# Loading the last w4 row of each partition by thirteen small transfers on ten or eight partitions each

## The chip, the cores and the metric

The kernel runs on one core of one Trainium2 chip. The metric is the device time of one execution in microseconds; for the kernel before, it was 1304.69 us, the median of three runs that lay between 1304.60 and 1304.81 us. A separate profiled execution gives the trace that is read below; its own time is in the table.

A core has engines that run side by side: TensorE (PE, matrix products), VectorE (DVE), ScalarE (ACT), GpSimd (POOL) and SyncE (SP, which here only issues transfers). Transfers between the large memory (HBM) and the on-chip memory (SBUF, 128 partitions) are carried by 16 DMA engines. Engines wait for each other, and for transfers, on semaphores; a transfer raises its semaphore by 16 when all of it has landed.

## The reference

One decoding step for four sequences, in float32. `x` is 4 x 512. It is normalised to `xn`, and the output is `x + A(xn) + B(xn)`:

```
xn  = layernorm(x)
q   = xn @ wq               -> 4 batches, 32 heads, 128 each
p   = softmax(q . k_cache * 128**-0.5)     k_cache: 4 x 32 x 4096 x 128
A   = (p @ v_cache) @ wo                   v_cache the same size, wo: 4096 x 512
B   = xn + gelu(LN(xn) @ w3) @ w4          w3: 512 x 1792, w4: 1792 x 512
```

(The reference's mixer with w1 and w2 shifts the sequence by one or two places; a sequence of length one is shifted out, so its term is zero and the kernel doesn't load those weights.) Nearly all of the bytes are the two caches: 256 MiB each. Every byte of them is read once.

## The kernel before, in words

**Tiling.** The caches are cut into 32 groups of four heads (`NG = 32`). A group is 8 MiB: each of the 128 partitions holds one contiguous row of 64 KB. SBUF has three such slots. `S1` and `S0` take K groups by turns, `S2` takes V groups. VectorE multiplies K by the query and sums (lines 343 to 347), ScalarE takes exponentials (line 245), TensorE multiplies the weights with V (line 201, recorded as line 108, the helper that issues every matrix product).

**The transfers.** SyncE issues all large loads, in one written order, on one DMA queue (lines 127 to 157). In the loop it waits until a slot is free and issues the next 8 MiB load into it. Each slot's wait ends while earlier loads are still under way, so loads queue up behind each other. After the loop it issues, in this order:

- line 146, w3 (3584 KB), and line 148, the rows 0 to 3 of w4 (1024 KB);
- lines 150 and 152, the last V group in two parts (3072 and 5120 KB), each after a wait for its part of the slot;
- line 153, the rows 4 to 13 of w4 (2560 KB);
- after one more wait (line 154, the K slot `S0` has been read), lines 155 to 157: wo in six pieces. wo has 32 rows of 2 KB in each partition, and the pieces hold 14, 8, 5, 3, 1 and 1 of them (`PIECES`, line 73).

**w4's layout.** w4 is 1792 x 512, so each partition holds 14 rows of 512 numbers, one behind the other in HBM: 28 KB for each partition, 2 KB for each row (`NF = 14`, line 147). Row 13 is the last row that this text speaks of.

**What waits for them.** TensorE, after the last group's products (block `pe_rest`, line 213), waits until both w4 loads have landed (line 215, 32 on semaphore `s_w4`), multiplies the gelu values with w4 (14 products, 28 records of the trace, lines 217 to 219), then forms the transposed attention output X (line 221), and then takes wo piece by piece: line 373 waits for piece n's own semaphore, and lines 374 to 382 multiply it. The first 27 rows of wo go through the accumulator `y`, rows 27 to 31 straight into `total`. When the last piece is through, VectorE and ScalarE copy `total` out (lines 391 and 393), and SyncE and ScalarE write the two halves of the result to HBM (line 396).

**x.** The input x (4 rows of 2 KB) is loaded at the start by ScalarE's own DMA queue, into four partitions (line 226). It is the only load of the kernel that goes to fewer than 128 partitions; the two result transfers read four partitions each.

Of the kernel before, what the change touches and what calls it, by code (L numbers as in the profile page):

```python
# [13 lines left out]
P = 128  # L14
# [6 lines left out]
def decode_block(ctx: ExitStack, tc: tile.TileContext, x, k, v, wq, wo, w3, w4, out):  # L21
# [5 lines left out]
    NF = F // P  # L27
# [39 lines left out]
    def sem(name):  # L67
        return tc.alloc_semaphore(name)

    def take(e, s, n=1):  # L70
        e.wait_ge(s, n).then_inc(s, -n)  # L71
# [2 lines left out]
    CUT = 27  # L74
    SUM = 30
    GF = 12
    s_x, s_v, s_q, s_w3, s_w4 = (sem(n) for n in ("sx", "sv", "sq", "sw3", "sw4"))
    s_k = [sem(f"sk{n}") for n in range(2)]
    s_wo = s_k + [s_x] + [sem(f"swo{n}") for n in range(3)]
# [16 lines left out]
    w4_sb = S1[:, NC * F:w34].rearrange("p (m n) -> p m n", m=NF)  # L96
# [10 lines left out]
    def mm(e, o, l, r, start, stop):  # L107
        return e.matmul(o, l, r, start=start, stop=stop)  # L108

    nc.vector.addr_align(128, offset=4, max_nops=0)  # L110
    with tc.tile_critical(no_gpsimd_drain=True), nc.Block(no_gpsimd_drain=True) as block:

        @block.sync
        def _(e):
            def src(flat, g):
                return flat[g] if isinstance(g, int) else flat[bass.ds(g, 1)].rearrange("g p r -> (g p) r")

            def load_k(g, n):
                e.dma_start(KS[n][:, :], src(kf, g)).then_inc(s_k[n], 16)

            def load_v(g):
                take(e, v_free)
                e.dma_start(S2[:, :], src(vf, g)).then_inc(s_v, 16)

            FIRST, REST = slice(0, GF * 4 * DH), slice(GF * 4 * DH, ROW)
            wq_r = wq.rearrange("(p c) n -> p (c n)", p=P)
            e.dma_start(S2[:, FIRST], wq_r[:, FIRST]).then_inc(s_v, 16)
            e.dma_start(S2[:, REST], wq_r[:, REST]).then_inc(s_q, 16)
            for half, s in ((slice(0, ROW // 2), s_k[0]), (slice(ROW // 2, ROW), s_kh)):
                e.dma_start(S1[:, half], kf[0][:, half]).then_inc(s, 16)  # L130
            e.wait_ge(d_T, 1)
            load_k(1, 1)
            with nc.Fori(0, NG, 2, engines=[ET.SP]) as g:
                load_v(g)
                take(e, k_free)
                e.br_lt(g, NG - 2, on_true="sp_more", on_false="sp_next")
                with nc.body("sp_more", valid_engines=[ET.SP]):
                    after = nc.s_assert_within(g + 2, None, NG - 2,
                                               skip_runtime_bounds_check_because="the last turn skips this block")
                    load_k(after, 0)  # L140
                    load_v(after - 1)
                    take(e, k_free)
                    load_k(after + 1, 1)
                    nc.br("sp_next", engines=[ET.SP])
                nc.switch_bb("sp_next")
            e.dma_start(w3_sb, w3.rearrange("(p c) f -> p c f", p=P)).then_inc(s_w3, 16)
            w4_r = w4.rearrange("(p m) n -> p m n", p=P)
            e.dma_start(w4_sb[:, 0:4, :], w4_r[:, 0:4, :]).then_inc(s_w4, 16)
            e.wait_ge(v_half, NG)
            e.dma_start(S2[:, FIRST], vf[NG - 1][:, FIRST]).then_inc(s_v, 16)  # L150
            take(e, v_free)
            e.dma_start(S2[:, REST], vf[NG - 1][:, REST]).then_inc(s_q, 16)
            e.dma_start(w4_sb[:, 4:NF, :], w4_r[:, 4:NF, :]).then_inc(s_w4, 16)
            take(e, k_free)
            wo_r = wo.rearrange("(p c) n -> p c n", p=P)
            for n, (c0, c1) in enumerate(PIECES):
                e.dma_start(wo_sb[:, c0:c1, :], wo_r[:, c0:c1, :]).then_inc(s_wo[n], 16)  # L157
# [20 lines left out]
        @block.tensor  # L178
        def _(e):
            pe = [ET.PE]  # L180
            zero = e.zero_reg
            e.br_lt(zero, 0, on_true="pe_near", on_false="pe_far")
            with nc.body("pe_near", valid_engines=pe):
                with nc.Fori(0, NG + 1, 1, engines=pe) as g:
                    e.br_lt(g, NG, on_true="pe_turn", on_false="pe_mlp")
                    with nc.body("pe_mlp", valid_engines=pe):
                        e.wait_ge(s_w3, 16)
                        for c in range(NC):
                            for t in range(4):
                                i = mm(e, pb[32 * t:32 * t + 32, :FT], x1T[:, c, :], w3_sb[:, c, t * FT:(t + 1) * FT],  # L190
                                       c == 0, c == NC - 1)
                        i.then_inc(p_a, 1)
                        nc.br("pe_turn", engines=pe)
                    nc.switch_bb("pe_turn")
                    take(e, s_v, 16)
                    take(e, a_p)
                    for n in range(G4):
                        if n == GF:
                            take(e, v_rest)
                        t = n % 4  # L200
                        i = mm(e, pv[32 * t:32 * t + 32, :], pw[:, n, :], V[:, n // 4, t], n < 4, n >= G4 - 4)
                        if n == GF - 1:
                            i.then_inc(v_half, 1)
                    i.then_inc(p_a, 1)
                    mm(e, oz[:, HG:2 * HG], ones[:, :], rs[:, :], True, True).then_inc(v_free, 1)
                    take(e, a_p)
                    for m in range(4):
                        i = mm(e, oz[:, 0:HG], os[:, m, :], sel[:, HG * m:HG * m + HG], m == 0, m == 3)
                    i.then_inc(p_a, 1)
                e.br_lt(zero, 0, on_true="pe_far", on_false="pe_rest")  # L210
            with nc.body("pe_far", valid_engines=pe):
                e.br_lt(zero, 0, on_true="pe_rest", on_false="pe_near")
            nc.switch_bb("pe_rest")
            mm(e, total[:, 0:P], ident[:, :], base[:, :], True, False)
            e.wait_ge(s_w4, 32)
            take(e, d_p)
            for m in range(NF):
                t = m % 4
                mm(e, y[32 * t:32 * t + 32, :], gT[:, 32 * m:32 * m + 32], w4_sb[:, m, :], m < 4, False)
            take(e, d_p)  # L220
            mm(e, pb[:, 0:P], perm[:, :], Xt[:, :], True, True).then_inc(p_d, 1)
# [148 lines left out]
    with tc.tile_critical(no_gpsimd_drain=True):  # L370
        e = nc.tensor
# [57 lines left out]
```

## Time and profile before

| | |
|---|---|
| median of three runs | 1304.69 us (1304.60 to 1304.81) |
| the profiled execution's own time | 1304.76 us |
| its span, first to last instruction | 1302.8 us |
| busy: VectorE / TensorE / ScalarE | 1167.5 / 371.5 / 107.5 us |
| moved by DMA | 561.05 MB, 431 GB/s over the span |
| share of the 16 DMA engines' time that SyncE's queue (q1) filled | 99.6% |
| mean granted TensorE clock | 0.625 of full speed |

The profiled execution took 1.96 us more than its span: what lies before the first and after the last instruction. The sums of the prediction are made against the profiled execution, which lies 0.07 us above the median.

Read the profile in this way. The page shows the span in forty slices, with the busy share of each engine and of the sixteen DMA engines together. A view of DMA by stretch counts the packets that begin in a stretch; one packet is one contiguous row moved for one partition, or the four bytes by which a DMA engine reports on the semaphore that its share of a transfer has landed. The chain of waits goes back from the last instruction to what released each step. The timeline lists instructions in order, with the idle time before them and what ended it.

### The profile page before, as it was taken

The numbers are of one execution on the slowest core, as the hardware profiler recorded it, in microseconds if no ns is written. First come the engines' busy times: TensorE is split into PE (matmuls) and PEld (weight loads), VectorE is DVE, ScalarE is ACT, GpSimd is POOL, SyncE is SP. The second block draws the span as 40 slices with busy tenths as digits, with TensorE's granted clock in tenths as the row PEclk, the third lists the DMA queues.
The fourth block names the chain that finished last, engine by engine and source line by source line (L and its number), as shares of the span: only waits on it lengthen the run. The fifth ranks groups of instructions, "written<-read, shape, count | busy, mean of one in ns | idle before, by whom it ended". The sixth has DMA issues, their size and how long they took to land. (4 is left out here: it accounts for less than half of the span.)

```text
span 1302.8 us, 7122 instructions
## 1 busy us (share of the span) xinstructions
PE 371.5 (29%) x2608; PEld 131.0 (10%) x2608; DVE 1167.5 (90%) x337; ACT 107.5 (8%) x330; POOL 2.5 (0%) x10
## 2 busy tenths in 40 slices
PE   3032123333113333212333212333311333321356
PEld 1010001111001111001111000111100111100112
DVE  4999999999999999999999999999999999999970
ACT  1000000000000000000000000000000000000010
POOL 0000000000000000000000000000000000000000
PEclk9565566666566666556666556666656666656678
DMA  9999999999999999999999999999999999999998
GB/s 402 436 449 421 449 421 449 421 439 429 425 445 421 449 421 449 421 449 421 449 421 445 425 437 431 425 445 421 449 421 449 421 449 421 447 423 445 425 430 344
DMA packets 11115, 561.05 MB, mean 431 GB/s; under 512 B 1244, under 2 KB 1252, under 8 KB 1640
## 3 DMA queue, kind: packets, MB, share of 16 engines
q1 hardware_dynamic: 11096, 561.00, 99.6%
q8 instruction: 2, 0.03, 0.0%
q14 instruction: 1, 0.01, 0.0%
q10 hardware_dynamic: 16, 0.01, 0.0%
HBM read 561.00 MB, written 0.01 MB: 431 GB/s over the span
## 5 line engine op out<-in xcount | busy, mean ns | idle before, releaser
L108 PE MATMUL ps<-slot,pw 128*32 128x512 f32 x2112 | 310.8, 753 | 905.5 <-PEq L71 905.5
L347 DVE TENSOR_REDUCE sc<-slot 128x128 f32<-128x16384 f32 x32 | 551.0, 17220 | 4.2
L343 DVE TENSOR_TENSOR slot<-slot,qb 128x8192 f32<-128x8192 f32 x32 | 278.1, 8692 | 60.8 <-DVEq L71 60.1
L345 DVE TENSOR_TENSOR slot<-slot,qb 128x8192 f32<-128x8192 f32 x32 | 277.9, 8684 | 1.1 <-DVEq L71 1.1
L108 PEld LDWEIGHTS ps<-slot,pw 128*32 128x32 f32 x2112 | 84.5, 134 | 1105.3 <-issue 1105.3
L233 ACT COPY os<-ps 128x512 f32<-128x512 f32 x33 | 19.3, 585 | 898.1 <-ACTq L71 898.1
L245 ACT ACTIVATE pw<-sc,st 32x128 f32<-32x128 f32 x128 | 67.4, 527 | 211.6 <-ACTq L71 210.4
L108 PE MATMUL ps<-sel,os 128*128 128x4 f32 x264 | 33.9, 252 | 18.6 <-PEq L71 18.6
L108 PEld LDWEIGHTS ps<-sel,os 128*128 128x128 f32 x264 | 31.9, 191 | 20.5 <-issue 20.5
L245 ACT ACTIVATION_READ_ACCUMULATOR pw<-sc,st 32x1 f32 x128 | 23.5, 184 | 0.0
L364 DVE RECIPROCAL rec<-OS 128x128 f32<-128x128 f32 x1 | 1.0, 952 | 15.5 <-DVEq L71 15.5
L349 DVE TENSOR_REDUCE st<-sc 128x1 f32<-128x128 f32 x32 | 9.2, 286 | 4.7
L108 PE MATMUL ps<-rs,ones 128*128 128x4 f32 x66 | 12.7, 263 | 0.0
L108 PEld LDWEIGHTS ps<-rs,ones 128*128 128x128 f32 x66 | 9.8, 188 | 27.7 <-issue 27.7
L337 DVE COPY qx<-Q 128x128 f32 x32 | 7.3, 227 | 5.0 <-issue 4.7
L391 DVE COPY res<-ps 64x128 f32<-64x128 f32 x1 | 0.3, 283 | 12.7 <-PE ps L108 12.7
L340 DVE STREAM_TRANSPOSE qb<-qx 128x128 f32<-128x128 f32 x32 | 10.0, 312 | 1.1
L108 PE MATMUL ps<-slot,X 128*4 128x512 f32 (+1 forms) x94 | 9.0, 457 | 3.9 <-DMA slot<-in_A_wo_dram 3.9
L253 ACT COPY OS<-ps 128x8 f32 x32 | 5.3, 165 | 43.8 <-ACTq L71 43.8
L351 DVE STREAM_TRANSPOSE mt<-mx 128x32 f32<-128x32 f32 x32 | 6.8, 211 | 1.1
L352 DVE TENSOR_REDUCE st<-mt 128x1 f32<-128x32 f32 x32 | 5.9, 186 | 1.1
L350 DVE COPY mx<-st 128x32 f32<-128x32 f32 x32 | 5.8, 181 | 1.1
(57 smaller groups left out, 39.3 us busy)
## 6 DMA issues: line engine op xcount, KB each, us to landing
slot<-in_A_k_cache_dram SPq DMA_DIRECT2D x2, 4096.0 KB, 36.0
slot<-in_A_wq_dram SPq DMA_DIRECT2D x1, 5120.0 KB, 22.4
slot<-in_A_v_cache_dram SPq DMA_DIRECT2D x1, 5120.0 KB, 20.5
slot<-in_B_w_dram SPq DMA_DIRECT2D x1, 3584.0 KB
slot<-in_A_wo_dram SPq DMA_DIRECT2D x1, 3584.0 KB, 29.4
slot<-in_A_wq_dram SPq DMA_DIRECT2D x1, 3072.0 KB, 10.7
slot<-in_A_v_cache_dram SPq DMA_DIRECT2D x1, 3072.0 KB, 13.1
slot<-in_B_w_dram SPq DMA_DIRECT2D x1, 2560.0 KB, 26.3
```

The costliest lines, as they stand in the source:

```text
L108: return e.matmul(o, l, r, start=start, stop=stop)
L233: return e.copy(os[:, :, :], pv[:, :].rearrange("p (m d) -> p m d", m=4)).then_inc(a_p, 1)
L245: i = e.activation(o, sc[r, :].rearrange("p (a w t) -> p a t w", w=4, t=4), AF.Exp, bias=st[r, 1:2], scale=1.0, accum_out=rs[r, h:h + 1])
L337: own(e.tensor_copy(qx[:, :].rearrange("p (h r) -> p h r", h=4), Q[:, bass.ds(g + n, 1), :].rearrange("p o h -> p (o h)").unsqueeze(2) .to ...
L340: own(e.transpose(qb[:, :], qx[:, :]))
L343: mark(e.tensor_tensor(out=K[:, :C // 2, :], in0=K[:, :C // 2, :], in1=qw, op=ALU.mult))
L345: own(e.tensor_tensor(out=K[:, C // 2:, :], in0=K[:, C // 2:, :], in1=qw, op=ALU.mult))
L347: mark(e.reduce_sum(sc[:, :], K, axis=AX.X))
L349: own(e.reduce_max(st[:, 0:1], sc[:, :], axis=AX.X))
L350: own(e.tensor_copy(mx[:, :], st[:, 0:1].to_broadcast([P, 32])))
L351: own(e.transpose(mt[:, :], mx[:, :]))
L352: e.tensor_reduce(st[:, 1:2], mt[:, :], axis=AX.X, op=ALU.max, negate=True).then_inc(d_a, 1)
```

## The change

The load of w4's rows 4 to 13 is cut in two. Rows 4 to 12 (18 KB for each partition) are loaded by one transfer as before. Row 13 (2 KB for each partition) is loaded by thirteen transfers behind it: twelve that each take ten partitions which lie twelve apart (partitions r, r + 12, ..., r + 108 for r = 0 to 11) and one that takes the partitions 120 to 127. All are issued by SyncE on the same queue and raise the same semaphore. TensorE waits for 32 + 16 x 13 = 240 on it instead of 32. Nothing else differs: the bytes, their places in SBUF and the arithmetic are the same.

```
+    LAST = (*(slice(r, 120, 12) for r in range(12)), slice(120, P))
...
-            e.dma_start(w4_sb[:, 4:NF, :], w4_r[:, 4:NF, :]).then_inc(s_w4, 16)
+            e.dma_start(w4_sb[:, 4:NF - 1, :], w4_r[:, 4:NF - 1, :]).then_inc(s_w4, 16)
+            for rows in LAST:
+                e.dma_start(w4_sb[rows, NF - 1, :], w4_r[rows, NF - 1, :]).then_inc(s_w4, 16)
...
-            e.wait_ge(s_w4, 32)
+            e.wait_ge(s_w4, 32 + 16 * len(LAST))
```

## The prediction, made before the change was run

> **What bounds the kernel now.** I read the page first, for the shares of the span:
>
> ```profile
> span 1302.8 us, 7122 instructions
> PE 371.5 (29%) x2608; PEld 131.0 (10%) x2608; DVE 1167.5 (90%) x337; ACT 107.5 (8%) x330; POOL 2.5 (0%) x10
> ...
> DMA  9999999999999999999999999999999999999998
> ...
> q1 hardware_dynamic: 11096, 561.00, 99.6%
> ```
>
> The DMA engines are full from one end to the other; VectorE, the busiest compute engine, has 10% to spare. So the time is that of the bytes on sixteen DMA engines, and a change counts if it changes the moment at which the last of them is done. The chain of waits, from 1259 us on, says the same of the end:
>
> ```profile
> 1259.43 36.57 DMA slot<-in_A_wo_dram
> ...
> 1296.04 1.88 PE ps L108 x10
> ...
> 1297.96 1.69 PE ps L108 x48
> ...
> 1299.67 0.28 DVE res L391
> ```
>
> TensorE takes wo as it lands, and 0.5 us after the last product the result goes out. The timeline shows where TensorE stands idle for a piece of wo:
>
> ```profile
> 1288.08 3.61 PE L108 MATMUL ps<-slot,X 128*4 128x512 f32 x28 [1.42 <-DMA slot<-in_A_wo_dram]
> ...
> 1296.04 0.12 PEld L108 LDWEIGHTS ps<-slot,X 128*4 128x4 f32 x8 [2.11 <-DMA slot<-in_A_wo_dram]
> ...
> 1297.96 0.55 PEld L108 LDWEIGHTS ps<-slot,X 128*4 128x4 f32 x24 [0.96 <-DMA slot<-in_A_wo_dram]
> ...
> 1299.20 0.12 PEld L108 LDWEIGHTS ps<-slot,X 128*4 128x4 f32 x8 [0.26 <-DMA slot<-in_A_wo_dram]
> ```
>
> It waits for every piece, for the last one until 1299.20. A shift of all landings therefore passes to the end in full, later without limit, earlier up to about 1.4 us (at 1288.08 TensorE had been idle that long; beyond it X itself would be late).
>
> A load has landed when the slowest of its sixteen shares has. I looked at the last stretch with 2 KB packets, first by DMA share, then by packets (from 1297.87 to 1298.72 us):
>
> ```profile
> 1297.30:1297.87 0.57, 0.57 (x2) 0.00 (x0) 0.00 (x0) 0.00 (x0) 0.00 (x0) 1.00 0.35 126
> 1297.87:1298.72 0.85, 0.82 (x29) 0.66 (x32) 0.00 (x0) 0.59 (x1) 0.00 (x0) 1.00 0.06 24
> ```
>
> ```profile
> DMA packets 12, 0.02 MB, mean 24 GB/s; under 512 B 2, under 2 KB 2, under 8 KB 12
> ...
> q1 hardware_dynamic: 12, 0.02, 6.3%
> ```
>
> A share of 0.06 of sixteen engines is one engine. For the last 0.85 us of the weights **one DMA engine works alone**, on ten 2 KB rows and two landing reports; the other fifteen are done by 1297.87. Why it is late stands at the start. The packets that begin from 1.94 to 2.75 us, then those in five stretches of 0.01 us (from 3.42, 4.83, 5.74, 6.65 and 7.57 us):
>
> ```profile
> q1 hardware_dynamic: 15, 0.37, 164.0%
> q8 instruction: 1, 0.02, 9.8%
> q14 instruction: 1, 0.01, 5.0%
> ```
>
> ```profile
> q1 hardware_dynamic: 1, 0.02, 886.2%
> ...
> q1 hardware_dynamic: 1, 0.02, 570.0%
> ...
> q1 hardware_dynamic: 1, 0.02, 570.0%
> ...
> q1 hardware_dynamic: 1, 0.02, 575.0%
> ...
> q1 hardware_dynamic: 1, 0.02, 570.0%
> ```
>
> Fifteen engines begin their first row of wq; the sixteenth moves instructions and begins its first row only at 3.42 us (this packet takes 886% of 16 x 0.01 us = 1.42 us, the next ones 0.91 us). Since the queue never runs dry, it keeps that delay for 1295 us. That it is the same engine at both ends is inferred, not shown.
>
> **The change part by part.**
>
> *Bytes per DMA engine.* Each of the sixteen had 8 rows of 20 KB of this load and now has 8 of 18 KB: 16 KB less. The rate, while V and w4 are loaded (1253.2 to 1274 us), is
>
> ```profile
> DMA packets 321, 8.95 MB, mean 430 GB/s; under 512 B 33, under 2 KB 33, under 8 KB 33
> ```
>
> 430 / 16 = 26.9 GB/s for an engine, so 16,384 B less is **-0.61 us on all sixteen**.
>
> *Who gets the 128 short rows.* The one load to few partitions that the trace shows is that of x (5.4 to 7.6 us):
>
> ```profile
> DMA packets 54, 1.14 MB, mean 518 GB/s; under 512 B 4, under 2 KB 4, under 8 KB 8
> ...
> q10 hardware_dynamic: 8, 0.01, 1.1%
> ```
>
> Four rows, four landing reports: four engines with one row each, not sixteen. By this nearest row I take ten engines with one row each for a load of ten partitions, eight for the last. On which engines a load begins, the trace doesn't show: I take the same first ten each time, so that eight engines get 13 rows, two get 12, and **six get none**. (The other bound, rows spread evenly, is a rival below.)
>
> *Price of a short row.* The lone engine gives it: 6.3% of 16 x 0.85 us is 0.857 us for ten rows with their reports, 0.086 us each. Lower bound, bytes alone at 26.9 GB/s: 0.076. Upper bound, the x rows: 1.1% of 16 x 2.2 us is 0.39 us for four, 0.097. So eight engines get 13 x 0.086 - 0.61 = +0.51 us (0.38 to 0.65), two get 12 x 0.086 - 0.61 = +0.42 (0.30 to 0.55), six get -0.61.
>
> *The end.* It turns on whether the late engine is one of the six. The four engines with an x row aren't it: an x packet pushes the next row of its engine back by 0.09 us, and the late engine's rows begin 0.91, 0.91 and 0.92 us apart all through the stretch with the x packets. If loads to few partitions begin on the same engine, the four are among the ten, and of the twelve engines left six are relieved, four get +0.51 and two +0.42. Six relieved is the largest of the three groups, and my forecast: the late engine is done 0.61 us sooner; the others, at least 0.85 us ahead of it, are then late by at most 0.51 - 0.85 = -0.34 against the old end. The end moves by -0.34 if the next-latest is one of the eight, up to -0.61 if all late ones are relieved. I take **-0.40**, nearer to the first, since ten of sixteen are loaded.
>
> *Issue.* SyncE issues thirteen more transfers between line 153 and the wait of line 154, with wo's six behind them:
>
> ```profile
> 1253.24 0.43 SPq L153 DMA_DIRECT2D slot<-in_B_w_dram  x1
> 1258.58 2.70 SPq L157 DMA_DIRECT2D slot<-in_A_wo_dram  x6
> 1299.98 0.35 SPq L396 DMA_DIRECT2D out_dram<-res  x1
> ```
>
> ```profile
> L226 ACTq DMA_DIRECT2D slot<-in_A_x_dram x1: 563/563/563, 1.6 to 1.6; - x1
> ```
>
> A transfer of four partitions costs 0.35 us on SyncE's queue and 0.56 us on ScalarE's; with the 0.04 us between issues, thirteen cost 5.1 to 7.8 us, and wo is issued from 1258.8 to 1261.5 us on instead of 1258.58. What hides it is the load of w4 ahead of wo, issued at 1253.24 and landed 26.3 us later, at 1279.5:
>
> ```profile
> DMA to landing us min/median/max: 26.3/26.3/26.3
> ...
> 1282.61 3.63 PE L108 MATMUL ps<-slot 128*32 128x512 f32 x28
> ```
>
> The engines reach wo some 18 us after its issue, so nothing of 0.2 to 2.9 us is seen; without that cover it would be paid in full. Nothing else is queued on SyncE until the result goes out at 1299.98. ScalarE's and GpSimd's queues aren't passed.
>
> *TensorE's wait on w4.* It now needs all fourteen loads. They land 1279.5 + 0.51 = 1280.0 us, 1280.2 at the upper bound; TensorE starts on w4 at 1282.61, after other work. Cost nothing with 2.4 us of cover; without it, X and wo's products behind it would be late.
>
> *Sum.* 1304.76 (the profiled execution) - 0.40 = 1304.36; the median stands 0.07 lower, so **1304.3 us**.
>
> **The rivals.**
>
> *The late engine is one of the ten* (0.40). Then it gets +0.42 or +0.51 and nothing covers it: 1304.7 + 0.5 = 1305.2 us (0.30 to 0.65, so 1305.0 to 1305.3). For it: ten of sixteen get more. Against it: only the x argument, which takes four of the ten away.
>
> *A load of ten rows uses one or two engines* (0.06), and this makes it slower. Sixty rows on each of two engines are 60 x 0.080 (bytes and a little) = 4.8 us, with the last load's row +0.09, less 0.61: +4.3; those engines are 0.85 to 1.4 us ahead of the late one, so about +3.0, 1307.7 us. On one engine, 120 rows: 9.6 + 0.7 for reports and the last row - 0.61 - 1.1 = +8.6, 1313.3 us. It decides from some 30 rows on one engine. For it: the trace shows four rows on four engines, never ten on ten. Against it: that same row.
>
> *The short rows spread evenly* (0.05): 8 x 0.086 - 0.61 = +0.08 on all sixteen, 1304.8 us: the change does nothing.
>
> *Each short load costs a pause of its own* (0.02). The result's 4 KB take at most 1302.8 - 1299.98 = 2.8 us from issue to the end; thirteen in a row would be +36 us, 1341 us. Against it: the wo pieces of 256 KB. From 1297.96 to 1299.20 two of them land: 1.24 us for 524,288 B, which at 430 GB/s are 1.22 us. Back-to-back loads leave no pause. [...]
>
> **How the numbers follow.** Forecast 0.47, then 0.40, 0.06, 0.05, 0.02. A difference under 0.2% (2.6 us) can't be told from none here; forecast, late-engine rival and even spread are all inside, 0.92, and the other two are slower, 0.08. For a gain over 2.6 us no engine has the room, as bytes are unchanged: 0.01, taken from the middle. The forecast's own range: 1304.1 (-0.61) to 1304.6 (0.65 - 0.85 = -0.20, with a margin). The range given reaches over the first rival too, and up to one more fetch of instructions on the late engine, since SyncE's program grows: 16 KB, +0.61: 1305.3 + 0.6 = 1305.9. Low: 1304.1 less the 0.1 by which runs differ. So 1303.9 to 1306.0.
>
> **What would show each step.** In the trace after: 2 KB packets and landing reports begin only at w4's end, 128 more of the one and 128 of the other, if ten rows go on ten engines; far fewer reports if on one or two. At the end, the stretch in which one engine works alone shrinks from 0.85 us to 0.5 or less if it was relieved, and grows to 1.2 or more if not. SyncE issues thirteen loads of about 0.4 us each, and wo begins at 1259 to 1261.5. TensorE starts on w4 within 0.1 us of 1282.6; an idle stretch there, ended by w4, makes the cover wrong. Wrong altogether I am if the time leaves 1303.9 to 1306.0: then either the rows lie on few engines, or short loads cost more than their bytes.

## The result, and the profile after

The changed kernel takes **1306.79 us** (median of 22 runs, 1305.55 to 1307.37) beside 1304.77 us before (22 runs, 1304.42 to 1305.10): the ratio is **1.0013, 95% interval 1.0007 to 1.0019**, so it is slower by some 0.1 to 0.2%. I had forecast 1304.3 us and a range up to 1306.0. The runs don't lie around one value: 9 of the 22 are at 1305.6 to 1306.0 us, 13 at 1306.7 to 1307.4. The profiled execution, 1305.73 us with a span of 1303.9 us, is of the lower group, 0.97 us above the profiled execution of before.

The page of the changed kernel:

```profile
span 1303.9 us, 7135 instructions
...
DMA packets 11372, 561.06 MB, mean 430 GB/s; under 512 B 1372, under 2 KB 1380, under 8 KB 1896
...
q1 hardware_dynamic: 11352, 561.00, 99.6%
```

There are 128 more packets under 512 B than before (1372 to 1244) and 256 more under 8 KB: 128 short rows with 128 landing reports, one engine for each row, as forecast. The queue is as full as before, for the same bytes and a longer time.

SyncE's issues in the timeline, and the thirteen and the six by line:

```profile
1253.64 0.43 SPq L154 DMA_DIRECT2D slot<-in_B_w_dram  x1
1254.12 9.72 SPq L156 DMA_DIRECT2D slot<-in_B_w_dram  x13
1263.96 10.97 SPq L160 DMA_DIRECT2D slot<-in_A_wo_dram  x6
```

```profile
L156 SPq DMA_DIRECT2D slot<-in_B_w_dram x13: 469/708/927, 1254.1 to 1263.4; - x13
```

```profile
L160 SPq DMA_DIRECT2D slot<-in_A_wo_dram x6: 353/432/4770, 1264.0 to 1270.2; - x6
```

An issue took 0.71 us, not the 0.35 to 0.56 that I had taken from the rows of before. One issue of wo stood for 4.77 us, and what is left of the 10.97 us says that another stood for some 4.3. The wo issues ended at 1274.9 instead of 1261.3. The engines reach wo's first row at 1277, so this is still hidden: even the last issue is 2 us ahead of that, where it was 16 us before.

What is not hidden shows in six microseconds, from 1277 to 1283, in which the short rows and the first rows of wo run. Before, and then after:

```profile
DMA packets 109, 2.58 MB, mean 429 GB/s; under 512 B 16, under 2 KB 16, under 8 KB 16
```

```profile
DMA packets 328, 2.12 MB, mean 354 GB/s; under 512 B 139, under 2 KB 139, under 8 KB 262
...
q1 hardware_dynamic: 328, 2.12, 106.2%
```

The DMA engines are busy all the time (106%, since packets count where they begin) and move 0.45 MB less. At 430 GB/s that is **1.05 us of all sixteen engines**, and the profiled executions differ by 0.97 us. In the middle of it, from 1277.40 to 1278.22 us, nothing begins but short rows and reports:

```profile
DMA packets 126, 0.13 MB, mean 155 GB/s; under 512 B 64, under 2 KB 64, under 8 KB 126
...
q1 hardware_dynamic: 126, 0.13, 68.5%
```

68.5% of 16 x 0.82 us is 8.99 us for 62 rows with their reports: **0.145 us for a row**, not 0.086. The long rows are slow as well. Three views of 0.01 us of the changed kernel (from 1276.82, 1277.31 and 1277.39 us), then one of 0.02 us of the kernel before (from 1279.02 us):

```profile
q1 hardware_dynamic: 1, 0.00, 52.5%
...
q1 hardware_dynamic: 3, 0.02, 674.4%
...
q1 hardware_dynamic: 1, 0.03, 1093.1%
...
q1 hardware_dynamic: 2, 0.03, 337.8%
```

The first short row of all takes 0.084 us (52.5% of 0.16), about the price that I had forecast. An 18 KB row of w4 with two reports takes 1.08 us, where 18,432 B at 26.9 GB/s are an estimated 0.69. A 28 KB row of wo takes 1.75 us; before, such a row and a report together took 1.08. The engine of this 28 KB row has no short rows: no engine can have had twelve of them, some 1.0 us at 0.084 us each, behind it 0.57 us after the first began. So the short rows also slow engines that carry none.

At the end of the span the waits of TensorE have moved as a whole (1296.04 to 1297.07, 1299.20 to 1300.22), and w4 is not waited for:

```profile
1283.01 3.63 PE L109 MATMUL ps<-slot 128*32 128x512 f32 x28
...
1297.07 0.12 PEld L109 LDWEIGHTS ps<-slot,X 128*4 128x4 f32 x8 [1.91 <-DMA slot<-in_A_wo_dram]
...
1300.22 0.12 PEld L109 LDWEIGHTS ps<-slot,X 128*4 128x4 f32 x8 [0.27 <-DMA slot<-in_A_wo_dram]
```

The windows of the last microseconds have no lone engine any more; several engines are still at work after 1299 us:

```profile
1297.00:1298.00 1.00, 0.93 (x9) 0.27 (x10) 0.00 (x0) 0.00 (x0) 0.00 (x0) 1.00 0.95 377
1298.00:1299.00 1.00, 1.00 (x10) 0.08 (x9) 0.00 (x0) 0.01 (x1) 0.00 (x0) 1.00 0.65 248
1299.00:1300.00 1.00, 1.00 (x40) 0.81 (x40) 0.00 (x0) 0.58 (x1) 0.00 (x0) 1.00 0.22 84
```

A share of 0.22 in the last one is 3.5 engines on average, where one engine was left before. In this execution the late engine seems to have been relieved indeed. From 1279.54 to 1279.56 us there begin

```profile
DMA packets 2, 0.03 MB, mean 1434 GB/s; under 512 B 1, under 2 KB 1, under 8 KB 1
```

a report and a 28 KB row of wo, right behind the last 18 KB row of all (begun at 1278.36): the engine that ends its long rows of w4 last has no short row. It gains nothing by that. The two rows that it writes last, the 18 KB row from 1277.31 us shown above and the one from 1278.36 us, which begins where the other ends, take 1.06 and 1.18 us instead of 0.69. Its first row of wo begins at 1279.55 us; before, the last engine began wo at 1279.03. That is 0.5 us later and not 0.61 us sooner.

### The profile page after: what moved, and what is told of

It is laid out like the page before. It is cut to its first block, busy times and chain, and to the rows that moved or that the text cites. A ratio compares the mean times of both kernels' runs of the same rounds, so it can differ in the third digit from the quotient of the medians.

```text
span 1303.9 us, 7135 instructions
## 1 busy us (share of the span) xinstructions
PE 368.1 (28%) x2608; PEld 130.6 (10%) x2608; DVE 1167.6 (90%) x337; ACT 107.6 (8%) x330; POOL 2.5 (0%) x10
## 2 busy tenths in 40 slices
DMA packets 11372, 561.06 MB, mean 430 GB/s; under 512 B 1372, under 2 KB 1380, under 8 KB 1896
## 5 line engine op out<-in xcount | busy, mean ns | idle before, releaser
L109 PE MATMUL ps<-slot,pw 128*32 128x512 f32 x2112 | 305.8, 743 | 910.9 <-PEq L71 910.9
```

## The experiments

The times are medians; the kernel before, run beside each of them, lay between 1304.70 and 1304.86 us. What a short row costs was tried first by where it goes, by how many reports stand behind it, and by where it comes from. All of these kernels change only `LAST`, the list of partitions, unless a diff says otherwise.

**The changed kernel again** (no edit).

> The changed kernel once more. Two things are open: why the thirteen short loads cost more than 0.086 us for a row, and why the changed kernel's runs fall in two groups (1305.6 to 1306.0 and 1306.7 to 1307.4 us). Theory A (the late DMA engine is another one from execution to execution): both groups appear again on one chip, about 1.1 us apart; where the trace is of the upper group, the late engine carries short rows, and where it is of the lower group, it carries none. Theory B (the late engine is fixed, and the groups come from somewhere else, such as the chip): one group alone on this chip, and the late engine the same in both groups' traces. Either way the stretch in which the short rows run moves about 260 GB/s with the DMA engines at about 100% busy.

Measured: 1306.81 us (1305.52 to 1307.38), ratio 1.0013 (1.0004 to 1.0023). The two groups came again, on one chip, with some runs between them (1306.27, 1306.30). So the chip doesn't make the groups.

**One load of 64 partitions, and eight loads of eight partitions that lie four apart.**

```
-    LAST = (*(slice(r, 120, 12) for r in range(12)), slice(120, P))
+    LAST = (slice(64, P), *(slice(h + r, h + r + 29, 4) for h in (0, 32) for r in range(4)))
```

> [...] The large load and the bytes are those of the changed kernel. [...] Theory R (a load with its landing report costs some 0.17 us on every engine that it uses, wherever it goes): the eight loads cost as many as in the next kernel, 8 x 0.17 + 4 x 0.08 - 0.61 = +1.1 on eight engines, and the end moves by +0.2 to +1.1.

Measured: 1305.84 us, ratio 1.0010 (1.0001 to 1.0019).

**Its twin, with the eight loads' partitions eight apart.** The pair asks whether it matters which partitions a load of eight takes.

```
+    LAST = (slice(64, P), *(slice(r, 64, 8) for r in range(8)))
```

> [...] Theory R: the same time and the same rows as its twin, within 0.2 us.

Measured: 1306.12 us, ratio 1.0011 (1.0002 to 1.0020). The same window of 1277 to 1283 us, first of the kernel with partitions four apart, then of this one:

```profile
DMA packets 296, 2.32 MB, mean 386 GB/s; under 512 B 96, under 2 KB 96, under 8 KB 224
```

```profile
DMA packets 292, 2.17 MB, mean 362 GB/s; under 512 B 96, under 2 KB 96, under 8 KB 224
```

As many rows and reports; 386 against 362 GB/s. The difference of the times, 0.3 us, is inside their intervals; theory R allowed 0.2. So the times settle nothing. The rows say more. Late in the stretch, a report and a short row in two views of 0.02 us, the first kernel from 1279.06 us and the second from 1279.22:

```profile
q1 hardware_dynamic: 2, 0.00, 29.1%
```

```profile
q1 hardware_dynamic: 2, 0.00, 50.0%
```

29.1% of 16 x 0.02 us is 0.093 us, 50.0% is 0.160. So late in the stretch a short row with its report is near its old price of 0.086 us in the first kernel and still dear in the second, in one execution of each. That speaks for a part played by the partitions that a load takes; why, no view shows.

**Neighbouring partitions.**

```
+    LAST = (*(slice(10 * r, 10 * r + 10) for r in range(12)), slice(120, P))
```

> The changed kernel with its thirteen loads over adjacent partitions: twelve of ten neighbours and one of eight. [...] Theory R: the same two groups as the changed kernel, 1305.7 and 1306.9 us. If rows that lie 344 KB apart in HBM were what is slow (theory H), these rows, 28 KB apart, would be faster: 1305 us or less.

Measured: 1306.00 us (1305.87 to 1307.53), ratio 1.0012 (1.0003 to 1.0021); the window moved

```profile
DMA packets 334, 2.08 MB, mean 346 GB/s; under 512 B 143, under 2 KB 143, under 8 KB 270
```

346 GB/s, hardly less than the changed kernel's 354: ten neighbouring partitions and ten that lie twelve apart make nearly the same stretch. The two groups that theory R expected are there. And rows that lie close in HBM are no faster (1306.00 us, where theory H gave 1305 or less).

**One load of 128 partitions, and two of 64.** These two tell most. Theory P, from here on, rests on an assumption of mine: that an engine writes the same partitions in every load of 128, and others in a smaller load. The trace numbers neither engines nor partitions, so no run shows it.

```
+    LAST = (slice(0, P),)
```

> [...] Theory P (short rows are slow because they go to partitions that other engines write): rows of 0.084 us and no change, 8 x 0.080 - 0.61 = +0.03, 1304.8 us. Theory T (what is slow is a landing report behind every row or two): 1304.8 us as well. If a 2 KB row in the middle of long ones were slow by itself: 8 x 0.17 - 0.61 = +0.75, 1305.5 us.

```
+    LAST = (slice(0, 64), slice(64, P))
```

> [...] Theory T: a fourth of the changed kernel's reports, so rows of 0.084 us and 1304.8 us.

Measured: 1304.75 us for the one load, ratio 1.0000 (0.9991 to 1.0009); 1305.85 us for the two, ratio 1.0008 (0.9999 to 1.0017), all eleven runs between 1305.32 and 1306.24. The window, for one load and then for two:

```profile
DMA packets 241, 2.56 MB, mean 427 GB/s; under 512 B 32, under 2 KB 32, under 8 KB 160
```

```profile
DMA packets 243, 2.16 MB, mean 360 GB/s; under 512 B 48, under 2 KB 48, under 8 KB 176
```

The same 128 rows, from the same places in HBM, with sixteen reports more: 427 becomes 360 GB/s, and 0.40 MB less, 0.93 us at 430 GB/s, stands beside 1.10 us in the time. What differs is that there are two loads, and that each covers half of the partitions. Whether other engines then carry a partition's row, no view shows. A 2 KB row between long ones is not slow by itself (427 GB/s with 128 of them), and few reports are enough for the whole loss of the lower group: theory T, which gave 1304.8 us for two loads, is out. SyncE's issues are not its cause: wo's six take 2.71 us in both kernels, as they did before. Theory R is out too: two loads at 0.17 us and six more rows at 0.08 on each engine, less 0.61, would be +0.2 us and not +1.1.

**Four loads of 128 partitions with a quarter of the row each.**

```
-    LAST = (*(slice(r, 120, 12) for r in range(12)), slice(120, P))
+    LAST = tuple(slice(n * D // 4, (n + 1) * D // 4) for n in range(4))
...
+            for cols in LAST:
+                e.dma_start(w4_sb[:, NF - 1, cols], w4_r[:, NF - 1, cols]).then_inc(s_w4, 16)
```

> [...] Theory P: no slow stretch; 32 rows of about 0.024 us on each engine - 0.61 = +0.15, 1304.9 us. Theory T: 64 reports in less than 1 us, denser than in the changed kernel, so the stretch slows down to 260 GB/s and the time is 1305.5 us or more.

Measured: 1305.28 us, ratio 1.0004 (0.9995 to 1.0013). The window:

```profile
DMA packets 671, 2.56 MB, mean 427 GB/s; under 512 B 79, under 2 KB 590, under 8 KB 590
```

64 reports and 512 rows, and as many bytes in the window as with the one load; so neither the number of loads nor that of reports makes the slow stretch. The 0.5 us in the time, for 0.15 expected, were not followed up; neither theory gives them.

**Three loads of forty and one of eight; then six of twenty and one of eight.** As many short rows, with 38 and with 68 reports instead of 128: ten for each of the longer loads and eight for the last, so again ten engines and eight, as I read the reports.

```
+    LAST = (*(slice(40 * r, 40 * r + 40) for r in range(3)), slice(120, P))
```

> Row 13 in three loads of forty neighbouring partitions and one of eight: the same ten and eight engines carry the same 12 or 13 short rows as in the changed kernel, with 38 reports instead of 128. Theory T: rows of 0.084 us; the late engine relieved gives -0.3 to -0.6, not relieved +0.4 to +0.5: 1304.3 or 1305.2 us, which is what I had predicted for the changed kernel. [...]

```
+    LAST = (*(slice(r, 120, 6) for r in range(6)), slice(120, P))
```

> [...] If the reports add their own part, in proportion to their number: 1305.6 + 1.2 x 30 / 90 = 1306.0 us, with a smaller part of the runs in the upper group than the changed kernel has.

Measured: 1305.59 us, ratio 1.0009 (1.0000 to 1.0018), and 1306.25 us, ratio 1.0011 (1.0002 to 1.0020). The windows, of forty and of twenty:

```profile
DMA packets 244, 2.27 MB, mean 378 GB/s; under 512 B 50, under 2 KB 50, under 8 KB 173
```

```profile
DMA packets 276, 2.27 MB, mean 378 GB/s; under 512 B 81, under 2 KB 81, under 8 KB 205
```

Both lose 0.3 MB, and their fastest runs, 1305.43 and 1305.29 us, are about those of the changed kernel, 1305.52. So the lower group costs some 0.7 us more than before with 38 reports as with 128. The number of runs in the upper group (1306.5 us and more, profiled executions left out) is larger with more reports in these kernels: 1 of 10 with 38, 4 of 10 with 68, 20 of 31 in the changed kernel with 128. But the other kernels with 128 reports have fewer again: 4 of 10 with neighbouring partitions, 3 of 10 in each of the two that follow (other places in HBM, thirteen semaphores); and the two kernels with eight loads, with 80 reports, have 2 of 10 each. The counts point to the reports and don't show it.

**Other places in HBM.**

```
-                e.dma_start(w4_sb[rows, NF - 1, :], w4_r[rows, NF - 1, :]).then_inc(s_w4, 16)
+                n = (rows.stop - rows.start + (rows.step or 1) - 1) // (rows.step or 1)
+                e.dma_start(w4_sb[rows, NF - 1, :], w4[10 * rows.start:10 * rows.start + n, :]).then_inc(s_w4, 16)
```

> The changed kernel, but each short load reads neighbouring rows of w4 in HBM (10 rows of 2 KB, one contiguous block of 20 KB) instead of rows 344 KB apart; it writes to the same partitions as the changed kernel. It leaves out w4's last row of each partition: other rows of w4 stand in its place. Theory P (where the rows go): the slow stretch of about 260 GB/s as before, rows of 0.13 us, 1305.6 to 1307.3 us. Theory H (where the rows come from): rows of 0.084 us and 1304.3 or 1305.2 us.

Measured: 1306.26 us (1305.46 to 1306.82), ratio 1.0010 (1.0001 to 1.0019), and for the one load of 128 partitions, read in the same way (`w4[rows, :]`),

> The kernel with one short load of 128 partitions, reading 128 neighbouring rows of w4 (256 KB in one block) instead of rows 28 KB apart. It leaves out w4's last row of each partition in the same way. Theory P: no slow stretch and 1304.8 us, as with the rows in their place. Theory H: the DMA engines read rows that others read in the large load, so the stretch slows down and the time is 1305.3 us or more.

1304.73 us, ratio 1.0000 (0.9990 to 1.0009). The windows of the two:

```profile
DMA packets 335, 2.16 MB, mean 360 GB/s; under 512 B 141, under 2 KB 141, under 8 KB 268
```

```profile
DMA packets 239, 2.59 MB, mean 431 GB/s; under 512 B 31, under 2 KB 31, under 8 KB 157
```

Where the rows come from makes no difference to the stretch. What is left is the shape of the load: 360 GB/s with thirteen loads of ten or eight partitions, 431 with one of 128.

**Thirteen semaphores.**

```
-                e.dma_start(w4_sb[rows, NF - 1, :], w4_r[rows, NF - 1, :]).then_inc(s_w4, 16)
+                e.dma_start(w4_sb[rows, NF - 1, :], w4_r[rows, NF - 1, :]).then_inc(s, 16)
...
-            e.wait_ge(s_w4, 32 + 16 * len(LAST))
+            e.wait_ge(s_w4, 32)
+            for s in s_l:
+                e.wait_ge(s, 16)
```

> The changed kernel, but each of the thirteen short loads raises a semaphore of its own, and TensorE waits for all of them. If reports are slow because 128 of them raise one semaphore: the landings follow the rows by 0.5 to 0.7 us throughout instead of up to 2 us, the upper group is gone, and the time is about that of the kernel with loads of forty, 1305.6 us. If a DMA engine lands its reports one after another, wherever they go: the same two groups as the changed kernel, 1305.7 and 1306.9 us, and the same landings.

Measured: 1305.87 us (1305.58 to 1306.92), ratio 1.0009 (1.0000 to 1.0018). The window is that of the changed kernel (360 GB/s), so the slow stretch has nothing to do with the semaphore. 3 of 10 runs lie at 1306.5 us or above instead of 20 of 31: perhaps fewer, too few runs to say.

**Loads of few partitions at the very end.** w4 as before; the last piece of wo in four loads, and in the change's thirteen.

```
+                for rows in LAST if c1 == WC else (slice(0, P),):
+                    e.dma_start(wo_sb[rows, c0:c1, :], wo_r[rows, c0:c1, :]).then_inc(s_wo[n], 16)
```

> The kernel before, with w4 loaded as before and only the last piece of wo (one 2 KB row for each partition) loaded by three loads of forty neighbouring partitions and one of eight: the first ten DMA engines carry 12 or 13 rows of it and six carry none, at a time when most engines have nothing else to write. If the late engine is always one of the six: it ends 0.64 us sooner, the loaded ones, 0.85 us ahead, get some 5 rows more than the 8 they had, 5 x 0.084 = +0.42, or up to 5 rows and a doubling in part where they still cross each other, so the time is 1304.2 to 1304.6 us in one group. If the late engine changes between executions: two groups, 1304.3 and 1305.2 us or more. If rows to other engines' partitions are slow at the very end too: one group at 1305 us or above.

> The same with the last piece of wo in the change's own thirteen loads. Late engine always one of the six: 1304.2 to 1304.6 us. Late engine changing: two groups, 1304.3 and 1305.2 us or more. Against the run with four loads it shows what thirteen loads cost at the end of the program: nothing, if only the partitions count; 0.3 us or more, if the loads or their reports do.

Measured: 1305.22 us (1304.72 to 1305.52) with four loads, ratio 1.0003 (0.9994 to 1.0012); 1307.08 us (1305.90 to 1307.63) with thirteen, ratio 1.0018 (1.0009 to 1.0027). Relieving six engines at the end pays nothing; one group at 1305 us or above was the outcome expected if the rows of such loads are slow there too. The thirteen loads show what so many small loads, or their reports, can cost. From 1298.56 to 1300.30 us this kernel's packets are

```profile
DMA packets 1, 0.02 MB, mean 9 GB/s; under 512 B 0, under 2 KB 0, under 8 KB 0
...
q8 instruction: 1, 0.02, 5.0%
```

nothing but instructions, yet TensorE gets the last piece only then:

```profile
1300.34 0.12 PEld L109 LDWEIGHTS ps<-slot,X 128*4 128x4 f32 x8 [0.95 <-DMA slot<-in_A_wo_dram]
```

All rows had been moved 1.7 us earlier. In the kernel before, the last row began before 1298.72 and TensorE had its piece at 1299.20, some 0.5 us after. With four loads TensorE didn't wait for the last piece at all. I take it that reports which stand one behind the other on an engine land late; no view shows them landing one by one. With w4 such a lag is hidden (TensorE comes to w4 at 1283.01); at the end of wo it is paid.

**Four more profiles of the changed kernel,** for one of the upper group.

> The changed kernel, one more profile. Theory A (the late engine changes from execution to execution): where the time is 1306.0 us or less, the late engine goes from its last 18 KB row straight to a 28 KB row of wo; where it is 1306.2 us or more, it goes to a 2 KB row. Theory B (always the same engine): the same kind of row in every profile of this kernel, whatever the time.

> As the run before it: one more profile of the changed kernel, with the same two expectations.

> The changed kernel, one more profile, for one of the upper group (1306.6 us or more). Theory A (the late engine changes): in a profile of the upper group the late engine goes on to a 2 KB row, and six engines finish early at the end. Theory B (always one of the six without short rows): five engines finish early at the end and the late one behind them, in every profile.

> As the run before it: one more profile of the changed kernel, with the same two expectations.

Measured: 1305.55, 1306.03, 1305.64 and 1305.46 us. With the two earlier ones, six profiled executions lie between 1305.46 and 1306.27 us: **none is of the upper group**. In the first (1305.73) the late engine was relieved; in the others rows of several engines end within the same few nanoseconds where it finishes w4, and I could not tell in each. So the upper group has no profile, and its 1.1 us have no cause here. With 20 of 31 runs in it when no profile was taken, six misses would be a chance of some 1 in 500; a profiled execution seems to stay out of that group, and the traces need not show what makes the median. That the late engine changes is not excluded for it; neither is a longer delay by reports, to which the counts above point without showing it.

## Why the prediction was wrong

It failed at **the price of a short row**, and at a term that the sum put at nothing: **what the short rows do to the long rows of all other engines**. The price was 0.086 us, with bounds of 0.076 and 0.097; in the middle of the stretch it was 0.145 us. I took it from the lone engine, beside which nothing ran, and from four x rows, beside which 518 GB/s were moved. With 0.145 us alone the sum would still have given only 13 x 0.145 - 0.61 - 0.85 = +0.43 us. The rest is in the long rows: 1.06 to 1.75 us where 0.69 to 1.07 were due (18,432 and 28,672 B at 26.9 GB/s, an estimate), and this on engines that carry no short row, which the sum had as the winners.

The sum assumed that DMA engines are independent, so that bytes moved from one to another cost as much there. The run with two loads of 64 partitions speaks against it: 128 rows, with a report from each of sixteen engines for each load, bring all sixteen engines down to 360 GB/s over 6 us, where one load of the same rows left 427. This holds for the lower group, some 1 us of the loss. The median lies in the upper group, another 1.1 us higher, and for that the failed step stays open.

*Bytes per engine, -0.61 us.* The six relieved engines lost their rows, but the slow stretch took more from all sixteen: 1.05 us in mean.

*Who gets the short rows.* Right as far as it shows: 128 reports, so one engine for a row in each load.

*The end.* In the profiled execution the late engine was, as far as it shows, among the six, the case that I had forecast. It made no gain: it came to wo 0.5 us later than before, since its own last two rows of w4 were slowed by 0.9 us together. The others, which should have ended 0.34 us before the old end, weren't done before it either: several engines were at work past 1299 us, where one had been left until 1298.72.

*Issue.* Under-priced (0.71 us each against 0.35 to 0.56, and wo issues of up to 4.77 us), but covered as said. Thirteen loads of neighbouring partitions were issued in 4.80 us instead of 9.72, so the price goes with the shape of the load.

*TensorE's wait on w4.* Right: none, at 1283.01 us.

*The rivals.* "The late engine is one of the ten" used the same price and would have been as wrong. The rival of few engines gave 1307.7 us, near the upper group, by a mechanism that did not happen: rows and reports are 128. The pause of its own for each load, to which I gave 0.02, is not there in that form (four loads more in the run with quarters cost 0.5 us in all), but short loads that stand at the end, with nothing behind them, did land late: the last piece of wo in thirteen loads reached TensorE 1.7 us after its last row. I had read from the two 256 KB pieces that back-to-back loads leave no pause; those have eight rows to a report, not one.

*The range.* Its upper end, 1306.0 us, was drawn with prices from undisturbed rows. The lower group lies inside, the median does not. The 0.92 for no difference beyond 0.2% came true with 0.13%, but by luck: neither the forecast nor the two rivals behind that number had the slow stretch or the two groups in them.

What stays open: the upper group and with it half of the loss at the median, which engine writes which partition in a load of fewer than 128, and why a load that covers fewer partitions is dear.

## What to carry to other kernels

In a full stream, split a load by columns over all 128 partitions, which cost nothing here as one load (0.5 us as four), and not by partitions, which cost 1.1 us for 256 KB in two loads. An engine that was late by 0.85 us couldn't be relieved here by giving its partitions to others in the middle of the stream. Price an operation from rows that ran beside the traffic that it will meet, not from rows that ran alone.

## What the runs showed of the hardware that I had not expected

How many partitions a load covers matters: 427 and 431 GB/s where 128 short rows went out in one load of 128 partitions, and 427 with four such loads of quarter rows; 346 to 386 where they went in loads of fewer, in the same six microseconds. Ten neighbouring partitions made nearly the same stretch as ten spread ones (346 against 354 GB/s). What makes the smaller loads dear, no view shows.

A price can depend on what runs beside it: the first short row took 0.084 us, those in the middle 0.145 with their reports, and a 28 KB row beside them 1.75 us, where one with a report had taken 1.08 before.

SyncE's issues can stand still: wo's six took 2.71 us behind one or two short loads, 10.97 behind the thirteen and 17.73 behind the four with quarter rows. What they wait for, no view shows. And the last load can land late if there is a report for each row: 1.7 us after the last row, in the run with thirteen loads at the end of wo.
